# A written-out order of 2017 pieces laid anew, with another choice of engines

## The chip, the cores and the metric

One core of a Trainium2 chip. Times are device microseconds of one execution of the program on that core; lower is better. Five engines run side by side, each with its own list of instructions: TensorE (PE, matmuls, its weight loads shown as PEld), VectorE (DVE), ScalarE (ACT), GpSimd (POOL) and SyncE (SP), which here issues nearly all transfers.

## The reference

An attention over pooled keys and values feeds a layer that mixes tokens and channels. Eight batches, eight heads of 64, 576 tokens, float32:

```python
k_p = k.reshape(B, H, Sp, pool, D).mean(axis=3)      # pool = 8, Sp = 72
v_p = v.reshape(B, H, Sp, pool, D).mean(axis=3)
attn = softmax(scale * q @ k_p^T)
x = (attn @ v_p), heads side by side                 # 8 x 576 x 512
theta = x @ w_theta
zr, zi = x * cos(theta), x * sin(theta)
y = w_tok_r @ zr + w_tok_i @ zi                      # over the 576 tokens
u = x + y
out = u + maximum(u @ w_ch, 0)
```

(The softmax and the names are shortened; the weights come as 64-bit floats, which the kernel reads as pairs of 32-bit words.)

## The kernel before

The work of each batch is cut into streams, which are Python generators. One `next` of a stream records one piece: a transfer, a group of matmuls, or an elementwise step. A table, `SCHEDULE`, is a long list of words. Each word names a stream, with a letter behind it where the piece may run on more than one engine: v for VectorE, g for POOL, a for ScalarE. The loop at the end of the function takes the words one after the other and calls `next`. As every engine works through its list in the order in which pieces were recorded, the table sets the order on all engines and on SP's transfers, and the letter sets the engine. Nothing else decides it: the tiles' buffers are fixed by name, and waits follow from who wrote and who reads them.

The streams, with the batch as first number:
- `w`, `W`: the token weights, from 64-bit words to float pairs (`wsrc_a`, `wsrc_b`), then turned on TensorE into `WTh` and `WTl` (a value and its rounding error). `h` and `c` do the same for the angle weights `th`, `tl` and the channel weights `chh`, `chl`.
- `k`, `K`, `Q`, `v`, `V`: loads of keys, queries and values, pooling, and layout. SP issues 8 transfers for a later batch's `Q` piece, 2 for a `v` piece.
- `S`: scores of one token tile, maximum (L758), exponential (L779), sum, and the normalised weights `en`. From batch 2 on VectorE writes 32x32 transposed blocks into `G`.
- `E`: 16 transfers from `G` to `eraw` (L868) complete the transposition of a group of two or three token tiles; then a rounded copy `eh`, copies `er`, their errors, and the error of `eraw` in place (L889 on VectorE, L190 on POOL).
- `X`: the attention's product with the values, one channel block of 128 (`pv`, L916, four matmuls), and the copy that empties its PSUM bank into `xT` (L927 on VectorE, L925 on ScalarE). Most of these use one bank, so the next product waits for the copy.
- `T`: angles of one token tile (`pt`, L964), sine and cosine on ScalarE (L985, L993), and `z` (L1002, L1004).
- `Z`: `zh` and the rounding error `zl` of one channel block of `z` (L1036 on VectorE, L190 on POOL). `M`: the mix over tokens (`py`, L1056, 27 matmuls), the sum `xT` (L1066), and `uh`, `ul` (L1073 on VectorE, L190 on POOL).
- `F`: the product with the channel weights (`pf`, L1089, 12 matmuls), L1096, a transpose into `R` (L1109), and 4 transfers to the output.

Elementwise work on POOL goes through a helper (lines 190 and 194), which cuts a piece of 512 or more elements in two. Copies of every kind have the lines of another helper, 205 for ScalarE and 207 for VectorE and POOL. ScalarE holds one table of functions at a time, and the program puts an ACT_TABLE_LOAD wherever the next function is not in it: an exponential after a sine, or the other way round.

Of the kernel before, what the change touches and what calls it, by code (L numbers as in the profile page):

```python
# [35 lines left out]
w3.0 w0.1v X0.0.0v S0.2v w2.0 w1.1 w0.1 S0.4 S0.3v S0.2 X0.0.1 Q1.0 S0.2a Q1.1 X0.0.1v k1.1 h3v S0.2 w0.1 S0.4 h3
S0.3g h3 S0.3 X0.0.3 w2.1 k1.2 S0.3a w0.1v X0.0.3v w1.1 h3v S0.4 W0 X0.0.2 S0.2a h2v w2.0 S0.4g w1.1a w2.0a S0.3 h2
S0.3a X0.0.2v h1v S0.4g S0.4 S0.4a h3 h1 S0.4 Q1.0 w1.0g S0.4v w2.0a W0a K1.1g X0.2.3 h3v w1.1a h3 Q1.1 X0.2.3v
X0.2.1 W0 X0.2.1v T0.0a T0.0v Q1.1a T0.1a W0 w2.1 T0.0 v1.0 W0a w1.1 Q1.3 w2.1a T0.0 w2.0 X0.2.0 T0.1v w2.0 w2.1v
T0.0 X0.2.2 W0 T0.0 Q1.0a X0.2.0v w3.1 w1.1 w2.1 Q1.2 K1.2g T0.0 w1.1v W1 V1.0v T0.1 Q1.3 w2.1 T0.0a X0.2.2v T0.0  # L40
# [45 lines left out]
X4.0.1v S4.4 M3.0.1 X4.0.2 K6.0g Q5.1 X4.0.2v M3.0.0 Q5.1 X4.0.3 M3.0.1 M3.0.0 S4.4v X4.0.3v Z3.1v M3.0.1 K5a V5.2v
S4.4v M3.0.1 S4.4 X4.0.0 M3.1.0 M3.1.0 k6.1 M3.0.0v X4.0.0v S5.2 M3.0.1a M3.1.1 T4.0v M3.1.1 M3.1.1 T4.1a S5.2
Z3.3a S5.2 Z3.3v S5.2 M3.1.0 S5.2v S5.2v M3.1.1 T4.0v F2.2.1 Z3.2v S5.3 T4.1g M3.1.0 Z3.2g E4.2 K6.1g T4.0 M3.0.0v
T4.0 M3.0.1g M3.2.0 T4.0 S5.3 S5.3 E4.2a M3.2.0 M3.1.1g T4.0 M3.2.1 S5.2 M3.1.0g M3.2.1 M3.2.1 S5.3 S5.4 S5.3g T4.0
# [1156 lines left out]
```

## Time and profile before

| | before |
|---|---|
| median of 3 runs (584.72 to 588.34) | 585.06 us |
| profiled execution, its own time | 587.04 us |
| its span, first to last instruction | 585.3 us |
| busy: TensorE, VectorE, ScalarE, POOL | 558.0, 466.9, 322.5, 324.7 us |
| TensorE's mean granted clock | 0.994 |
| transfers | 57.84 MB, 99 GB/s |

A busy share tells how full an engine is, not what waits for what. For that the profile infers, for each instruction that began after idle time, who released it. TensorE's matmuls are pipelined: a matmul lasts longer than the distance to the next one, so times of work are read from runs of matmuls back to back. [...]

### The profile page before, as it was taken

To read this page: it belongs to the slowest core of one execution; us is meant where nothing else is said; L and a number is where in the kernel's file an instruction comes from. 1 tells how busy PE (TensorE), PEld (TensorE's weight loads), DVE (VectorE), ACT (ScalarE), POOL (GpSimd) and SP (SyncE) were. 2 spreads that over 40 slices of the span, in tenths; PEclk is the share of its full clock that TensorE was granted. 3 is DMA by queue.
4 is the path that set the end of the run, shared out by engine and by line. 5 is a ranking of instruction groups with operands and counts; after the bars stand their busy time and mean duration, and the time that the engine had idled before them with its cause. 6 is when DMAs were issued, how large, how long until landed. Compare 5 with 4: busy or idle time off the path is not lost.

```text
span 585.3 us, 11574 instructions
## 1 busy us (share of the span) xinstructions
PE 558.0 (95%) x4102; PEld 520.1 (89%) x4102; DVE 466.9 (80%) x931; ACT 322.5 (55%) x660; POOL 324.7 (55%) x476
## 2 busy tenths in 40 slices
PE   8899989998999988999999998999999999999997
PEld 7766989986899887899989897999899999999996
DVE  3989989898989888878887987888887987447345
ACT  3688958877952676536833562627633556425100
POOL 6435642455572586576746567276936785551250
PEclk9999989999999999999999998999999999999999
DMA  9966212367465667543365465316556151212115
GB/s 301 280 206 159 76 46 82 62 125 143 95 117 104 152 122 131 112 100 65 96 119 99 81 103 94 73 30 113 103 87 112 31 85 15 41 27 43 21 21 81
DMA packets 235385, 57.84 MB, mean 99 GB/s; under 512 B 223424, under 2 KB 223936, under 8 KB 235328
## 3 DMA queue, kind: packets, MB, share of 16 engines
q1 hardware_dynamic: 230464, 56.52, 46.8%
q10 hardware_dynamic: 4864, 0.59, 0.7%
q8 instruction: 32, 0.52, 0.4%
q14 instruction: 25, 0.20, 0.1%
HBM read 37.81 MB, written 9.44 MB: 81 GB/s over the span
## 4 chain that ended last, share of the span: by engine, by line
PE 45%; DVE 17%; SPq 11%; POOL 9%; ACT 8%; DMA 5%; issue 5%; DVEq 0%; POOLq 0%; ACTq 0%
PE py L1056 20%; SPq L868 8%; PE pt L964 8%; PE pf L1089 6%; PE pv L916 3%; SPq L601 3%; DMA vprst<-in_v_dram 2%; PE s L724 2%; DMA eraw<-G 1%; DMA qsst<-in_q_dram 1%; DVE qT L606 1%; POOL xl L190 1%; DVE xT L927 1%; DVE mx L758 1%; PE warm L308 1%
## 5 line engine op out<-in xcount | busy, mean ns | idle before, releaser
L1056 PE MATMUL py<-WTh,zh 128*128 128x288 f32 x576 | 83.3, 291 | 2.0 <-ACT zh L205 1.4
L1056 PE MATMUL py<-WTh,zl 128*128 128x288 f32 x576 | 81.8, 289 | 0.9 <-DVE xT L1066 0.5
L1056 PE MATMUL py<-WTl,zh 128*128 128x288 f32 x576 | 82.3, 287 | 0.0
L1056 PEld LDWEIGHTS py<-WTh,zh 128*128 128x128 f32 x576 | 75.5, 191 | 3.2 <-ACT zh L205 1.9
L1056 PEld LDWEIGHTS py<-WTh,zl 128*128 128x128 f32 x576 | 74.7, 189 | 1.9 <-POOL zl L190 0.8
L1056 PEld LDWEIGHTS py<-WTl,zh 128*128 128x128 f32 x576 | 75.1, 189 | 0.2
L190 POOL TENSOR_TENSOR zl<-z,zh 128x256 fp32r<-128x256 f32 (+2 forms) x57 | 44.5, 812 | 28.7 <-ACT zh L205 20.7
L970 ACT ACTIVATE g<-pt,c_magic 128x512 f32<-128x512 f32 x35 | 24.0, 685 | 64.8 <-PE pt L964 41.8
L190 POOL TENSOR_TENSOR ul<-xT,uh 128x288 fp32r<-128x288 f32 x37 | 32.2, 879 | 34.8 <-ACT uh L205 30.7
L1066 DVE TENSOR_TENSOR xT<-py,xT 128x288 f32<-128x288 f32 x64 | 28.5, 447 | 27.4 <-PE py L1056 27.2
L205 ACT CAST zh<-z 128x1152 fp32r<-128x1152 f32 (+1 forms) x29 | 30.8, 1075 | 28.6 <-PE py L1056 24.1
L1089 PE MATMUL pf<-uh,chh 128*128 128x288 f32 x256 | 43.6, 293 | 0.1
L190 POOL TENSOR_TENSOR en<-e_eps,ri 128x256 f32<-128x256 f32 (+3 forms) x62 | 31.5, 529 | 20.5 <-DVE ri L783 9.0
L1089 PE MATMUL pf<-ul,chh 128*128 128x288 f32 x256 | 42.1, 286 | 0.7 <-POOL ul L190 0.7
L724 PE MATMUL s<-kpT,qT 128*128 128x144 f32 x256 | 39.3, 295 | 3.2 <-DVE qT L207 1.5
L190 POOL TENSOR_TENSOR xl<-xT,xh 128x256 fp32r<-128x256 f32 x46 | 33.6, 751 | 15.5 <-ACT xh L205 10.7
L1089 PE MATMUL pf<-uh,chl 128*128 128x288 f32 x256 | 41.8, 286 | 0.0
L964 PE MATMUL pt<-th,xh 128*128 128x512 f32 x148 | 39.5, 389 | 2.2 <-DVE g L972 0.9
L724 PEld LDWEIGHTS s<-kpT,qT 128*128 128x128 f32 x256 | 34.8, 194 | 5.1 <-DVE qT L606 1.1
L964 PE MATMUL pt<-tl,xh 128*128 128x512 f32 x148 | 38.0, 379 | 0.0
L964 PE MATMUL pt<-th,xl 128*128 128x512 f32 x148 | 38.0, 379 | 0.0
L1089 PEld LDWEIGHTS pf<-uh,chh 128*128 128x128 f32 x256 | 36.1, 189 | 1.5 <-DVE xT L1096 0.5
(266 smaller groups left out, 1409.8 us busy)
## 6 DMA issues: line engine op xcount, KB each, us to landing
out_dram<-R SPq DMA_DIRECT2D x112, 72.0 KB, 2.2
kpst<-in_k_dram SPq DMA_DIRECT2D x15, 512.0 KB, 3.9
vpst<-in_v_dram SPq DMA_DIRECT2D x28, 256.0 KB, 3.7
qsst<-in_q_dram SPq DMA_DIRECT2D x96, 72.0 KB, 2.3
eraw<-G SPq DMA_DIRECT2D x96, 60.0 KB, 2.2
eraw<-G SPq DMA_DIRECT2D x96, 40.0 KB, 2.0
WTh_st<-in_moe_w_theta_dram SPq DMA_DIRECT2D x4, 512.0 KB, 8.3
wcraw<-in_moe_w_ch_dram SPq DMA_DIRECT2D x4, 512.0 KB, 3.3
```

Source lines behind the costliest of these rows:

```text
L190: nc.gpsimd.tensor_tensor(out[:, r], a[:, r], b[:, r], op)
L205: nc.scalar.copy(out, src)
L308: nc.tensor.matmul(p[:, 0:P], ident, ident, start=True, stop=True)
L601: nc.sync.dma_start(st[32 * i : 32 * i + 32, S * c : S * c + S].rearrange("p (x a) -> p x a", a=32), q[b, 4 * j + 2 * c + i // 2].rearrang ...
L724: nc.tensor.matmul(scs[c // 2][:n, 2 * SP * (c % 2) : 2 * SP * (c % 2 + 1)], qT[:, c, t0 : t0 + n], kpT[:, c, :], start=True, stop=True,)
L868: nc.sync.dma_start(blocks(Ex, jj, i), blocks(Gx, i, jj))
L916: nc.tensor.matmul(as_written(pv[:, :gn]) if pair else pv[:, :gn], l, by_turns(r) if pair else r, start=i == 0, stop=i == len(terms) - 1,)
L964: nc.tensor.matmul(as_written(pt), l[:, c, :], by_turns(r[:, c, :]), start=i == 0, stop=i == 11)
L970: nc.scalar.activation(halves(g), in_order(pt), AF.Identity, bias=c_magic)
L1056: nc.tensor.matmul(as_written(py[:, :n]), l[:, kk, :], by_turns(r[:, kk, t]), start=i == 0, stop=i == 3 * NK - 1,)
L1066: nc.vector.tensor_tensor(halves(u), in_order(py[:, :n]), halves(u), ALU.add)
L1089: nc.tensor.matmul(as_written(pv[:, :n]), l[:, kk, o], by_turns(uhl[r][:, kk, t]), start=i == 0, stop=i == 11,)
```

## The change

Only the table changes. The 2017 words are the same pieces; their order is another, and for 331 pieces the letter. The table is two lines shorter, so line numbers behind it are lower by 2 (L190 is L188 after). In counting the costs from which the new table was made, operations of VectorE and of POOL on SBUF were taken to exclude each other. The first line before and after:

```diff
-D k0.0 w0.0 K0.0 k0.1 K0.1 h0 w0.0 w0.0v w0.0g w0.0 K0.0a k0.2 K0.2 Q0.0 K0.2v h0 h0g K0.1v h0v h0 h1 w1.0 K0 K0a
...
+w0.0 w0.0 D k0.1 h0 k0.0 w0.0a k0.2 h0 w0.0v h0v K0.1 w0.0 K0.0 h0v h1 K0.0a K0.2 Q0.0 h2 K0.1a Q0.0 K0 Q0.1 w0.1 h0
...
```

Copies that empty the attention's banks (`X`) go from 57 on VectorE and 7 on ScalarE to 16 and 48. The `zl` pieces on POOL go from 57 to 77, on VectorE from 36 to 26. The error of `eraw` in 3 of the 12 `E` streams goes from POOL to VectorE.

POOL, at the end of the token weights. `wsrc_b` is the second float of a weight, `wcts` the channel weights' buffers, `wpow` a scratch buffer, `vpst` and `vp` values being pooled, and `Vl` their rounding error. Before:

```order
L190 TENSOR_TENSOR vpst1_1_860<-vpst1_1_860 128x256 x2
L190 TENSOR_TENSOR vpst1_1_860<-vpst1_1_860 128x2x128
L190 TENSOR_TENSOR vp1_688<-vpst1_1_860 128x128
L388 MEMSET wpow_115 128x512
L194 TENSOR_SCALAR wpow_115<-wcts0_898 128x256 x2
L190 TENSOR_TENSOR wsrc_b_155<-wsrc_b_155,wpow_115 128x288 x2
L190 TENSOR_TENSOR wcts0_898<-wcts0_898 128x256 x2
```

After:

```order
L188 TENSOR_TENSOR wsrc_b_120<-wsrc_b_120,wpow_115 128x288 x2
L386 MEMSET wpow_115 128x512
L188 TENSOR_TENSOR wsrc_b_120<-wsrc_b_120,eraw0_114 128x288 x2
L188 TENSOR_TENSOR wsrc_b_120<-wsrc_b_120,wpow_115 128x288 x2
L188 TENSOR_TENSOR Vl_916<-vp1_694,Vh_103 64x4x64 x2
L188 TENSOR_TENSOR wcts0_860<-wcts0_860 128x256 x2
L205 CAST chh_958<-wcts0_860 128x512
```

The two TENSOR_SCALAR ahead of the last `wsrc_b` have left POOL, the last three pieces of `wsrc_b` stand together, and a copy to `chh` has come in behind them.

POOL, the `E` stream of batch 5's second group (tokens from 256 on); `kprst` and `kpr` are keys of batch 6 being pooled, `vrx` and `Vr` the last value rows of batch 5. Before:

```order
L207 CAST eh5_256_4335<-eraw5_256_4334 128x1280
L190 TENSOR_TENSOR Vr5_4473<-vrx5_4327,mask_84 96x256 x2
L207 CAST er5_256_4336<-eraw5_256_4334 32x320 x4
L190 TENSOR_TENSOR kprst6_4382<-kprst6_4382 64x256
L190 TENSOR_TENSOR kprst6_4382<-kprst6_4382 64x128
L190 TENSOR_TENSOR kpr6_4513<-kprst6_4382 64x64
L190 TENSOR_TENSOR er5_256_4336<-eraw5_256_4334,er5_256_4336 32x320 x2
L190 TENSOR_TENSOR eraw5_256_4334<-eraw5_256_4334,eh5_256_4335 128x2x320 x2
```

After:

```order
L205 CAST eh5_256_4453<-eraw5_256_4452 128x1280
L188 TENSOR_TENSOR er5_256_4454<-eraw5_256_4452,er5_256_4454 32x320 x2
L188 TENSOR_TENSOR vrx5_4429<-vpr5_4031,vrh5_4430 32x64 x2
L188 TENSOR_TENSOR Vr5_4562<-vrx5_4429,mask_84 96x256 x2
L188 TENSOR_TENSOR eraw5_256_4452<-eraw5_256_4452,eh5_256_4453 128x2x320 x2
```

The four copies of `er` are on ScalarE now, the three sums of keys stand earlier, and two pieces of `vrx` have come in between.

SP, from the transfers of the `E` stream before that one (`eraw4`) to its own (`eraw5`). Before:

```order
L868 DMA eraw4_256_4051<-G_101 32x15x32 x16
L601 DMA qsst6_0_4224<-in_q_dram 32x18x32 x8
L1124 DMA out_0_dram<-R2_3_3780 32x18x32 x4
L515 DMA vpst6_0_4269<-in_v_dram 64x2x512 x2
L868 DMA eraw5_256_4334<-G_101 32x15x32 x16
```

After:

```order
L866 DMA eraw4_256_4057<-G_101 32x15x32 x16
L522 DMA kprst6_4177<-in_k_dram 64x512
L510 DMA kpst6_1_4256<-in_k_dram 128x2x512
L599 DMA qsst6_0_4356<-in_q_dram 32x18x32 x8
L1122 DMA out_0_dram<-R2_3_3876 32x18x32 x4
L1122 DMA out_0_dram<-R2_2_3837 32x18x32 x4
L513 DMA vpst6_0_4406<-in_v_dram 64x2x512 x2
L866 DMA eraw5_256_4452<-G_101 32x15x32 x16
```

Two loads of keys and four transfers to the output have come in between, 20 issues in place of 14.

ScalarE, the sine and cosine of batch 3's tile 1 (`g` the angle, `sn` the sine, `e_eps` the exponential of a softmax). Before:

```order
L970 ACTIVATE g3_1_3514<-pt3_1_3497,c_magic_88 128x512
L985 ACTIVATE sn3_1_3532<-g3_1_3514 128x512
L205 CAST uh2_3241<-xT2_2179 128x288
L988 ACTIVATE g3_1_3514<-g3_1_3514 128x512
L993 ACTIVATE g3_1_3514<-g3_1_3514,c_cos_92 128x512
```

After:

```order
L968 ACTIVATE g3_1_3502<-pt3_1_3473,c_magic_88 128x512
L983 ACTIVATE sn3_1_3541<-g3_1_3502 128x512
L986 ACTIVATE g3_1_3502<-g3_1_3502 128x512
L777 ACT_TABLE_LOAD
L777 ACTIVATE e_eps_99<-e_eps_99 128x8x72
L991 ACT_TABLE_LOAD
L991 ACTIVATE g3_1_3502<-g3_1_3502,c_cos_92 128x512
```

An exponential with its table has come between the two sines, and the sines' table is loaded again behind it. The same stands at tiles 0 and 1 of batch 4.

## Rows read from the trace of the kernel before

**Rows 1.** The page: the span, and busy time of each engine (us, share, instructions).

```profile
span 585.3 us, 11574 instructions
...
PE 558.0 (95%) x4102; PEld 520.1 (89%) x4102; DVE 466.9 (80%) x931; ACT 322.5 (55%) x660; POOL 324.7 (55%) x476
```

**Rows 2.** One stretch: its length, busy us of each engine, granted clock, DMA share.

```profile
15.00:240.00 225.00, 210.40 (x1497) 187.44 (x1498) 202.35 (x404) 163.39 (x411) 119.22 (x184) 0.99 0.57 126
```

**Rows 3.** Waits of TensorE, whole span: who for whom, total us, times, longest.

```profile
PE pv L916 <- DVE xT L927: 3.0, 3, 1.7
...
PE pv L916 <- POOL eraw L190: 2.1, 1, 2.1
...
PE wt L451 <- POOL wsrc_b L190: 1.4, 2, 0.9
```

**Rows 4.** Two stretches of 6 us, columns as in Rows 2.

```profile
76.00:82.00 6.00, 4.68 (x26) 4.22 (x26) 4.52 (x11) 3.17 (x9) 3.33 (x4) 0.72 0.27 90
356.00:362.00 6.00, 4.50 (x20) 4.06 (x21) 3.89 (x8) 1.34 (x4) 5.41 (x8) 0.72 0.32 49
```

**Rows 5.** Order of time, POOL from 72 to 78 us: start, us, engine, line, what.

```profile
72.75 0.53 POOL L388 MEMSET wpow<- 128x512 int32 x1 [1.24 <-DVE wpow L368]
...
73.36 2.16 POOL L194 TENSOR_SCALAR wpow<-wcts 128x256 f16<-128x256 f32 x2
...
75.61 2.31 POOL L190 TENSOR_TENSOR wsrc_b<-wsrc_b,wpow 128x288 fp32r<-128x288 f32 x2
```

**Rows 6.** Order of time, issues of the DMA queue, 316 to 345 us.

```profile
316.92 4.40 SPq L601 DMA_DIRECT2D qsst<-in_q_dram  x8
...
323.62 1.35 SPq L515 DMA_DIRECT2D vpst<-in_v_dram  x2
332.75 11.92 SPq L868 DMA_DIRECT2D eraw<-G  x16
```

**Rows 7.** Order of time, POOL, 346 to 358 us.

```profile
346.48 1.25 POOL L207 CAST eh<-eraw 128x1280 fp32r<-128x1280 f32 x1 [3.49 <-PE pf L1089]
...
348.82 1.92 POOL L207 CAST er<-eraw 32x320 fp32r<-32x320 f32 x4
350.81 1.25 POOL L190 TENSOR_TENSOR kprst<-kprst 64x256 f32<-64x256 f32 x2
...
354.40 3.04 POOL L190 TENSOR_TENSOR eraw<-eraw,eh 128x640 fp32r<-128x640 f32 x2
```

**Rows 8.** Order of time, TensorE, 226 to 229 us.

```profile
226.73 0.40 PE L916 MATMUL pv<-eh,Vh 128*128 128x320 f32 x1 [1.01 <-ACT eh L205]
...
228.26 0.40 PE L916 MATMUL pv<-eraw,Vh 128*128 128x320 f32 x1 [0.99 <-DVE eraw L889]
```

**Rows 9.** Chain that ended last: start, us, runs of matmuls back to back.

```profile
145.40 2.59 PE pt L964 x12
...
255.25 1.10 PE py L1056 x9
```

**Rows 10.** Groups: line, engine, what, count | busy us, mean ns | idle before.

```profile
L190 POOL TENSOR_TENSOR zl<-z,zh 128x256 fp32r<-128x256 f32 (+2 forms) x57 | 44.5, 812 | 28.7 <-ACT zh L205 20.7 <-DVE zh L207 5.4 <-PE py L1056 2.1
...
L1066 DVE TENSOR_TENSOR xT<-py,xT 128x288 f32<-128x288 f32 x64 | 28.5, 447 | 27.4 <-PE py L1056 27.2
...
L1036 DVE TENSOR_TENSOR zl<-z,zh 128x640 fp32r<-128x640 f32 (+1 forms) x36 | 26.1, 766 | 1.3 <-ACT zh L205 1.3
...
L927 DVE TENSOR_SCALAR xT<-pv 128x256 f32<-128x256 f32 (+1 forms) x57 | 25.3, 446 | 13.4 <-PE pv L916 12.7
L1109 DVE STREAM_TRANSPOSE R<-xT 128x288 f32<-128x288 f32 x56 | 24.9, 461 | 0.4
...
L985 ACT ACT_TABLE_LOAD x18 | 23.1, 1283 | 0.3
...
L1073 DVE TENSOR_TENSOR ul<-xT,uh 128x288 fp32r<-128x288 f32 x27 | 15.0, 566 | 0.1
...
L925 ACT ACTIVATE xT<-pv 128x320 f32<-128x320 f32 (+1 forms) x7 | 2.9, 420 | 6.6 <-PE pv L916 3.8 <-DVE mx L758 2.8
```

More of the change, by code (lines that the diff above doesn't have):

```diff
@@ L36 @@
[L36 to L40, printed above, removed]
@@ L86 @@
[L86 to L89, printed above, removed]
-E4.2a T4.0a E4.2v T4.0 S5.3g K6 M3.2.1 S5.4 T4.1 M3.2.0 E4.2g M3.1.1g M3.2.0 X4.2.0 S5.4 Q6.0 M3.3.0 X4.2.0v F2.3.1
@@ new lines @@
+X2.0.3 X2.0.3a S2.4 v3.1 K3a V3.2g M1.1.1 Z1.2g X2.0.0 Q3.1 X2.0.0a T2.0a T2.0v Z1.2v T2.1a M1.1.1 M1.1.1 S3.2 M1.1.1
+M1.0.1 T2.0 Z1.3a V3.1g E2.2 M1.1.1g S3.2 S3.2 k4.0 T2.1g M1.0.1v M1.2.0 T2.0 S3.2 M1.3.0 S3.2g T2.0 Z1.3v M1.3.0
+E2.2a S3.2v M1.0.0a M1.2.0 k4.2 S3.3 M1.2.0 S3.3 E2.2g M1.2.0 S3.3 E2.2g S3.2 M1.3.0 Q4.0 T2.0 M1.1.1g T2.1 M1.3.0
+F0.3.1 T2.0 F0.2.1 E2.2v S3.3 X2.2.0 T2.0a S3.3g S3.3v S3.4 T2.0 M1.2.1 S3.4 M1.0.0g M1.3.1 T2.0 X2.2.0a X2.2.2 S3.0
+S3.3 K4.2g M1.3.1 K4.0g X2.2.2v S3.4 S3.4 k4.1 T2.0 M1.2.0a M1.1.0g X2.2.3 T2.1 S3.4v T2.1 M1.3.1 S3.4g S3.4 X2.2.3a
@@ new lines @@
+T3.2 V4g T3.2 T3.2 Q5.1 F2.0.1 E4.0g E4.0g K5a T3.3 T3.3 F2.3.0 T3.3 v5.2 F2.1.0 S4.3g S4.3g T3.3 T3.3a F2.3.0 T3.3
+F2.2.1 F2.2.0 F2.1.1 T3.3 K5 F2.0.1 T3.3 V5.1g F2.1.1 F2.2.1 Z3.0a F2.2.0 E4.0g Z3.0g S4.3 S4.4 F2.3.1 M3.0.0 F2.2.1
+M3.0.0 S4.4 F2.3.1 F2.2.0 S4.4 X4.0.1 F2.0.1 Z3.1g M3.0.0 F2.3.0 F2.3.1 M3.0.1 Q5.1 k6.0 X4.0.1a K5a X4.0.2 X4.0.2v
+S5.2 S4.4g K6.0g S4.4g S4.4 M3.0.0 S5.2 M3.0.1 X4.0.3 X4.0.3a M3.0.1 M3.0.1 S5.2 Z3.1g X4.0.0 M3.1.0 M3.1.0 M3.1.1
+X4.0.0v M3.1.0 T4.0a T4.1v Z3.3v M3.1.1 M3.1.1 T4.1g T4.0g S5.3 V5.2g S5.2 Z3.2a S5.2g T4.0 E4.2 Z3.3v M3.1.0 S5.2g
@@ new lines @@
+Z3.2g M3.2.0 S5.3 M3.0.1v S5.3 S5.3 T4.0 T4.0 M3.2.0 S5.2 M3.2.0 E4.2v S5.3v E4.2a S5.4 M3.1.1 E4.2g S5.3g T4.1 M3.2.1
+E4.2v T4.0 k6.2 S5.4 X4.2.0 S5.0 T4.0 S5.3 M3.2.1 T4.0a X4.2.0v M3.1.0a X4.2.2 S5.4 M3.2.0 S5.4 X4.2.2v M3.2.1 S5.4v
+S5.4g M3.0.0a T4.0 S5.4 X4.2.3 S5.0 M3.3.0 k6.1 K6.1g M3.1.0v M3.0.1g X4.2.3a M3.2.1 X4.2.1 X4.2.1a M3.3.0 T4.2a
+M3.3.0 M3.2.1v X4.2.3a T4.3g T4.0 M3.0.0v T4.0 S5.0 M3.3.1 M3.3.0 M3.2.0a M3.3.1 T4.1 S5.0 T4.2g M3.2.1g M3.2.0v V5a
+T4.1 M3.3.0v S5.1 M3.1.1v M3.3.1 S5.0v M3.3.0v Q6.0 M3.3.1 S5.0v S5.1 F3.0.0 T4.1 F2.3.1 T4.1 S5.1 F2.2.1 K6.2g
@@ new lines @@
+M3.3.1a M3.1.1v v6.0 Q6.0 T4.1v T4.1 M3.3.1g F3.3.0 T4.1 V5g V5 F3.0.0 T4.3g T4.2 E5.2 T4.1 K6 T4.2 E5.2g F3.3.0 K6v
+F3.1.1 T4.2 T4.2 E5.2a T4.2 F3.0.1 F3.1.1 E5.2g F3.0.0 V5g F3.0.1 Q6.1 F3.0.1 S5.0 F3.0.1 F3.1.0 F3.1.0 F3.1.0 V5g
+F3.1.1 F3.1.1 T4.2a F3.3.1 T4.3 S5.1 T4.2 F3.3.1 T4.2 T4.2 F3.2.0 E5.2g F3.3.1 T4.3 Q6.1 F3.2.1 X5.2.2 T4.3 F3.2.0
+F3.3.0 F3.2.0 T4.3 K6 T4.3 F3.2.1 S5.1g T4.3a K6a F3.2.1 S5.1g S5.1 X5.2.2a X5.2.0 X5.2.1 X5.2.3 T4.3 X5.2.0a V6.0g
+T4.3 X5.2.1v X5.2.3a X5.2.3v T4.3 S6.0 T4.4a T4.4g Z4.0a Z4.0v S6.0 v6.1 T4.4 Z4.0v S6.0 E5.0 T4.4 M4.0.0 S6.0 Q7.0
@@ new lines @@
+k7.2 T5.0 M4.3.0 S6.3 S6.2v M4.3.1g T5.0v T5.1 M4.2.0 T5.0 T5.0 M4.3.0 T5.0 S6.3 T5.1 S6.3 M4.2.0 M4.2.1g S6.4 T5.1
+M4.3.1v M4.1.1v K7.1v M4.0.1v M4.2.0 T5.3a F4.1.1 M4.2.0 M4.2.0g T5.1 M4.2.0g T5.1 T5.1a T5.2 T5.1 V6g M4.0.0g F4.0.1
+T5.1 F4.1.1 K7 M4.3.0a T5.1 M4.3.0g V6 E6.0 v7.0 T5.2 Q7.0 T5.2 F4.0.1 T5.2 T5.3g T5.2 E6.0a F4.0.0 T5.2a F3.2.1 S6.2
+T5.2 T5.4g T5.2 S6.3 F4.0.0 T5.3 S6.3g E6.0a T5.2 E6.0g S6.3v F4.0.0 Q7.1 K7a F4.1.0 F4.3.1 F4.1.1 T5.3 T5.3 V6g
+F4.1.0 T5.3 T5.3 F4.0.1 V6g T5.3a F4.1.0 F4.3.1 F4.2.0 T5.3 K7.2g T5.3 T5.3 Z5.0a F4.2.1 F4.2.0 S6.3 F4.2.1 S6.4
@@ new lines @@
+F4.0.1 E6.0v S6.4 F4.3.0 K7 F4.3.0 F4.1.1 F4.2.1 F4.3.0 F4.2.0 Z5.0g K7a M5.0.0 M5.0.0 Z5.1g X6.0.2 S6.4 F4.3.1
+X6.0.2a M5.0.1 M5.0.1 S6.4v S6.4g M5.0.1 v7.2 S6.4 X6.0.1 Q7.1 Z5.1g M5.0.0 X6.0.1a X6.0.0 M5.0.1 S7.2 X6.0.0a M5.0.1g
+Z5.3g M5.0.0 X6.0.3 S7.2 X6.0.3a M5.1.0 F4.2.1 M5.1.1 S7.2 M5.1.1 Z5.3g T6.1g M5.1.0 S7.3 T6.0v S7.2 V7.0g V7.2g
+M5.0.1g S7.2v M5.1.0 M5.1.0 T6.0g M5.1.1 S7.2v M5.3.1 S7.3 E6.2 Z5.2a S7.3 S7.3 Z5.2g M5.3.1 E6.2a M5.1.0a M5.1.1
+F4.3.1 M5.3.1 T6.0 E6.2a M5.3.1 T6.1v S7.2 S7.3v M5.3.1v M5.3.0 S7.4 v7.1 S7.3g E6.2g M5.2.1 M5.2.1 M5.3.1v E6.2v
@@ new lines @@
+T6.1 T6.2 E7.2v S7.0g T6.2 F5.3.1 T6.2 F5.3.1 T6.2 T6.2a F5.3.0 F5.2.1 X7.2.3 F5.3.1 F5.3.0 T6.2 T6.3 X7.2.3v X7.2.1
+X7.2.1a T6.2 X7.2.2 F5.2.1 T6.2 T6.3 X7.2.0 X7.2.0a X7.2.2v T6.3 T6.3 X7.2.3v T6.3 T6.3a T6.4v T6.3 T6.4g S7.1 T6.3
+S7.0 T7.3a T6.3 Z6.0a Z6.0g T7.3g S7.1 T6.4 T6.4 T7.2a T6.4 T6.4 T6.4 T6.4v M6.0.0 T6.4 T6.4 Z6.0g S7.1 T7.2v T6.4
+M6.0.0 Z6.0g T7.3 Z6.1a M6.0.0 Z6.0v M6.0.1 M6.0.1 Z6.0g T7.3 S7.1 T7.3 T7.3 S7.1g T7.3 M6.0.1 S7.1g S7.1 M6.0.1
+M6.0.0 M6.0.0 T7.2 E7.0 M6.1.0 M6.0.1 Z6.1v M6.0.1g M6.1.0 Z6.3a M6.0.0v T7.3v M6.1.1 E7.0a M6.1.1 M6.1.0 Z6.3v M6.1.0
@@ L136 @@
+F7.3.1 F7.1.1 F7.1.1 F7.2.1 F7.1.1 F7.0.0 F7.2.1 F7.2.1 F7.2.0 F7.3.1 F7.3.0 F7.2.0 F7.2.0 F7.1.0 F7.2.1 F7.1.1 F7.2.0
+F7.3.0 F7.3.0 F7.1.0 F7.3.0 F7.1.0 F7.1.0
 """
```

159 lines of the change are left out of this document (65 added, 94 removed).

## The prediction

> **What bounds the kernel now.** Read the page's busy times first [rows 1]: TensorE is busy 558.0 of 585.3 us, so all that a new order can win is in the 27.3 us in which it stands, and in what the clock loses. No matmul is added or removed. VectorE comes next with 80%, ScalarE and POOL have 55% each. Then read where the idle time lies, in the stretches [rows 2]: from 15 to 240 us TensorE stands 14.6 us (225.00 less 210.40), and VectorE is busy 202.35 of 225.00, 90%, far above its mean. That part is held by both. Third, the waits of TensorE by releaser [rows 3]: none is over 3.0 us in total. They are many small late hand-overs: the attention's next product waits for the copy that empties its bank (VectorE, L927) and for the rounding error of the turned attention weights (`eraw`, by POOL here), and the turning of the token weights waits for POOL's `wsrc_b`. [...]
>
> What else the rows show: of two VectorE operations of one size, 128x288, the one with an input from PSUM takes 447 ns and the one with both inputs from SBUF 566 ns (L1066 and L1073) [rows 10]. [...]
>
> **The change part by part.** 2017 words stay 2017 words; what changes is their order and 331 letters. Counted in the built programs, VectorE's instructions go from 931 to 876, POOL's from 472 to 513, ScalarE's from 580 to 608, with ACT_TABLE_LOADs from 38 to 42.
>
> (a) The last token weights. Before, POOL clears a buffer (0.53 us) and makes two half tiles for the channel weights (2.16 us), and only then the last `wsrc_b` halves, 2.31 us [rows 5], for which TensorE waits 1.4 us [rows 3]; then comes the slow clock. After, the two half tiles go to ScalarE, and between the word for the last `wsrc_b` and the first word that turns it there are 18 warm-up matmuls, 16 of the previous turning and 8 transposes on TensorE, where before there were none. They are smaller than the 128x288 ones of 0.122 us [rows 9], so at most 42 × 0.122 = 5.1 us of cover, for a piece of 2.3. What is late next is the previous turning (W3): behind its last piece (`w3.1`) no matmul stands ahead of it. I take the whole of it: −1.4 −1.7 = **−3.1**; between −3.1 and nothing.
>
> (b) Turned attention weights of batch 3, second group (E3.2). TensorE waits 1.01 us for `eh` and 0.99 us for `eraw` [rows 8]. Between the last word of the softmax that feeds the turning and the first product, TensorE's own work was 48 `pf`, 24 `pt`, and 20 small ones; after, 96 `pf`, 24 `pt`, 18 `py` and 20 small ones. A matmul of 128x288 takes 1.10/9 = 0.122 us and one of `pt` 2.59/12 = 0.216 us [rows 9]. So 48 and 18 more are 66 × 0.122 = 8.1 us of cover more, against 2.0 of wait: **−2.0**; bounds −2.0 and nothing, if the DMA queue comes later by as much.
>
> (c) Batch 5, second group (E5.2). TensorE waits 2.1 us for POOL's `eraw` [rows 3] and loses 1.7 by the clock [rows 4]. The chain: 16 transfers issued in 11.92 us [rows 6], then POOL alone from 346.48 to 357.44 [rows 7]. On POOL the copies of `er` (1.92) go to ScalarE and the sums of `kprst` (1.25) go ahead of it; two small pieces come in, unpriced. On TensorE 27 `py` more stand in between, 27 × 0.122 = 3.3 us, and 12 small ones, at as much 1.4: 4.7 us more cover. On the DMA queue, 20 issues stand between this stream's transfers and those of the E stream before it, where 14 stood: 6 more, at 4.40/8 = 0.55 us each 3.3 us [rows 6]. Before, the queue stood idle 7.8 us (from 323.62 + 1.35 to 332.75) until the softmax was done, so they fit in, if the keys' load at their head finds its buffer free early. Then nothing of the wait is left (2.1 − 4.7 − 1.9 − 1.2 < 0). If it does not, all 20 issues, 11.0 us, fall behind the softmax, and the wait grows to 2.1 + 11.0 − 4.7 − 1.9 − 1.2 = 5.3 us. Bounds: −3.8 and +3.2. The idle 7.8 us make the first the nearer one; I take half of its gain: **−1.9**.
>
> (d) Emptying the attention's banks. 41 of VectorE's 57 copies go to ScalarE: 41 × 0.446 = 18.3 us off the fuller engine, 41 × 0.420 = 17.2 us on one that is busy 55% [rows 1, 10]. TensorE waits 3.0 us for them [rows 3]. On ScalarE they stand behind casts and table loads as well, so I take half: **−1.5**, from −3.0 to nothing.
>
> (e) Four more table loads. Each is 1.283 us [rows 10]. Three come because an exponential is put between the two sines of one tile (T3.1, T4.0, T4.1). Cover: ScalarE is idle 45% of the time, and these tiles' `z` is wanted later. All on the path would be 5.1 us, none 0; I take half of one load, **+0.7**.
>
> (f) More rounding errors on POOL. `zl` pieces on POOL go from 57 to 77, on VectorE from 36 to 26: five more channel blocks. One takes POOL 4 × 0.812 = 3.2 us, VectorE 2 × 0.766 = 1.5 us [rows 10]. The product first does 18 matmuls without `zl`, 18 × 0.122 = 2.2 us of cover, so 1.0 us can show in each: up to 5.2, down to 0. No wait on `zl` is among the larger ones of before although 57 pieces were there, so I take a quarter: **+1.3**.
>
> (g) Late places of its own. [...] Another order will have some too that I can't name; I charge half of one: **+1.9**, from 0 to two of them, 6.9.
>
> Sum: −3.1 −2.0 −1.9 −1.5 +0.7 +1.3 +1.9 = −4.6 us. The profiled execution's span is 585.3 us and its own time 587.04, 1.7 us around the span; that gives 580.7 and 582.4. The median of the runs shown is 585.06, 2.0 below the profiled one; with the same −4.6 it becomes **580.4 us**.
>
> **The rivals.**
> VectorE's relief comes through. Weighted with the durations of before, VectorE's list sums to some 20 us less, 18 of them in (d), and the fuller part of the kernel is 15 to 240 us. If VectorE is what TensorE waits for there, two thirds of the 14.6 us of idle time go, 9.7, with the clock's 1.7 and (c)'s 1.9; less 2.0 for (e) and (f): −11.3, 573.8 us. For it: 90% busy. Against it: the rows of waits name POOL and ScalarE too, and POOL is handed 41 instructions.
>
> The waits only change places. TensorE's waits are spread over many releasers, and a new order draws all of them anew; an order that also keeps apart operations that the rows show not to disturb each other (transposes) gives away freedom for nothing. Then the change does not do what it says, and the time is 585 us, give or take 2.
>
> POOL becomes the late engine: slower. It gets 20 `zl`, 12 `vpst` and 3 `ul` pieces more, each about twice as long as on VectorE. [...] The trace agrees, 3.2 us against 1.5 for a block. The place is the product of the channel blocks: all five of (f) show, 5.2 us, and two of them are long enough to take the clock down, 2 × 1.7; (b), (c) and (d) are lost since their chains run through POOL, (a) stays, (e) adds 0.7: 5.2 + 3.4 + 0.7 − 3.1 = +6.2, 591.3 us. It decides once POOL starts a `zl` more than the 2.2 us of cover less its own 3.2 allow, that is at once in these blocks. Against it: POOL's share rises only from 55% to about 60%.
>
> **How the numbers follow.** Forecast (−8 to −2) 0.45; VectorE's relief 0.20; waits change places 0.22; POOL late 0.13. About 1% of this kernel, 5.9 us, is what a measurement can tell from no change: faster means under 579.2, slower over 590.9. Faster: all of the relief, and 0.20 of the forecast's 0.45, since 580.4 lies close to the line: 0.40. Slower: 0.12 of POOL's 0.13. Same: 0.48. The range, from the relief's 573.8 to just under POOL's 591.3, is 573.5 to 590.0, with 2 in 10 left out, more of it above. The forecast's own range is 577 to 583.
>
> **What would show it.** After: TensorE idle near 23 us instead of 27.3. (a) no wait for `wsrc_b` of over 0.5 and a clock of 1.00 around the last turning. (b) no wait for `eraw` before the product of batch 3's second group. (c) no wait of over 1 us at batch 5's, the clock not down, and its transfers issued as soon as the softmax is done. (d) waits for L927's copy under 1.5, none as long for ScalarE's L923. (e) `g` of T3.1 to T4.1 late, TensorE not. (f) waits for `zl` under 1.5 in sum. The prediction is wrong if VectorE's busy time does not fall, if a gap of 2 us opens at E5.2 behind the DMA queue, or if more than two falls of the clock are seen between 15 and 560 us.

## The result, and the profile after

| | before | after |
|---|---|---|
| median, 13 executions each | 585.87 us | 578.60 us |
| ratio, 95% interval | | 0.9873, 0.985 to 0.9896 |
| again, later (21 and 9 executions) | 584.54 us | 579.94 us; 0.9915, 0.9885 to 0.9945 |
| profiled execution, its own time | 587.04 us | 575.52 us |
| its span | 585.3 us | 573.7 us |
| busy: TensorE, VectorE, ScalarE, POOL | 558.0, 466.9, 322.5, 324.7 us | 550.3, 467.5, 328.6, 357.2 us |
| TensorE's mean granted clock | 0.994 | 0.998 |

The change makes the kernel 4.6 to 7.3 us faster, about 1%. (Ratios leave disturbed executions out, so they can differ a little from those of the medians.) The profiled execution is the fastest of its 13, and in it the clock did not fall before the last matmul (1.00 in every stretch up to 567.0 us, 0.84 behind it); over 22 executions the mean granted clock is 0.992, over 50 of the kernel before 0.9935. So the clock, which gives 3.4 us between the two profiles, gives nothing between the medians.

The page after, beside [rows 1]:

```profile
span 573.7 us, 11562 instructions
...
PE 550.3 (96%) x4102; PEld 516.0 (90%) x4102; DVE 467.5 (81%) x876; ACT 328.6 (57%) x688; POOL 357.2 (62%) x517
```

TensorE stands 23.5 us in place of 27.2 (unrounded; the page's rounded figures give 23.4 and 27.3). VectorE has 55 instructions fewer and is busy as long as before; that is explained below. The stretches of [rows 2] and of the first row of [rows 4], in the same columns:

```profile
15.00:240.00 225.00, 216.11 (x1580) 195.18 (x1580) 204.56 (x391) 173.48 (x435) 148.61 (x214) 1.00 0.62 129
76.00:82.00 6.00, 4.55 (x39) 4.17 (x38) 5.80 (x14) 4.81 (x8) 2.29 (x4) 1.00 0.08 29
```

From 15 to 240 us TensorE stands 8.9 us in place of 14.6. From 76 to 82 us the clock stays up, but TensorE still stands 1.45 us. The waits of TensorE, in the columns of [rows 3], say for what:

```profile
PE py L1054 <- ACT zh L203: 2.5, 3, 1.5
PE pv L914 <- ACT xT L923: 2.2, 5, 0.7
PE pt L962 <- ACT xh L203: 1.7, 2, 1.2
...
PE s L722 <- DVE qT L604: 1.3, 1, 1.3
PE pq L627 <- DMA early<-in_q_dram: 1.3, 1, 1.3
PE pv L914 <- DVE eraw L887: 1.1, 1, 1.1
PE kpp L566 <- DMA kpst<-in_k_dram: 0.8, 1, 0.8
PE wt L446 <- DVE WTl L457: 0.7, 1, 0.7
...
PE py L1054 <- POOL zl L188: 0.2, 1, 0.2
```

The three releasers of [rows 3] are gone: no `wsrc_b`, no `eraw` by POOL, no bank copy of VectorE. New places of 1 to 1.5 us stand in the list instead: the cast `zh` at 77 us, `xh` at 131, `qT` at 417, `eraw` by VectorE at 439, a first load of queries at 19.

The account of the 11.5 us (unrounded) between the two spans, the time behind the last matmul (the tail) apart:

| | before | after | |
|---|---|---|---|
| waits that steps (a) to (d) name (1.4, 2.0, 2.1, 3.0) | 8.5 | 2.2 | −6.3 |
| all other idle time of TensorE | 14.4 | 14.5 | +0.1 |
| lost to a low clock before the last matmul | 3.4 | 0 | −3.4 |
| tail | 4.3 | 6.8 | +2.5 |
| TensorE's busy time without the clock (558.0 − 3.4; 550.3) | 554.6 | 550.3 | −4.3 |

The last line is short stalls which the profile shows as busy, since no matmul was added or removed: matmuls overlap in it (in the kernel before one of `py` lasts 287 to 291 ns in the mean, and back to back they come 0.122 us apart). They aren't in the waits, but the trace has them by tile: counted without the clock, the attention's product `pv` makes 1.8 us of them, 1.6 in the first matmul of a product, the one that needs an emptied bank; `pe` makes 0.9, `s` and `pf` 0.7 each. The idle time falls in the same place. The two groups of `pv` that wait, before and then after, in the columns of [rows 10]:

```profile
L916 PE MATMUL pv<-eh,Vh 128*128 128x256 f32 (+1 forms) x56 | 18.1, 324 | 4.8 <-DVE xT L927 3.0 <-ACT eh L205 1.0 <-DVE er L836 0.7
L916 PE MATMUL pv<-eraw,Vh 128*128 128x256 f32 (+1 forms) x56 | 16.5, 295 | 4.3 <-DVE eraw L889 2.2 <-POOL eraw L190 2.1
```

```profile
L914 PE MATMUL pv<-eh,Vh 128*128 128x256 f32 (+1 forms) x56 | 17.6, 315 | 2.3 <-ACT xT L923 2.2
L914 PE MATMUL pv<-eraw,Vh 128*128 128x256 f32 (+1 forms) x56 | 16.2, 289 | 1.1 <-DVE eraw L887 1.1
```

In front of these two the idle time falls from 9.1 to 3.4 us. That is 5.7 of the 6.2 us by which TensorE's idle time before its last matmul falls (22.9 to 16.7).

### The profile page after: what moved, and what is told of

The parts are those of the page before. It is cut to its first block, busy times and chain, and to the rows that moved or that the text cites. A ratio compares the mean times of both kernels' runs of the same rounds, so it can differ in the third digit from the quotient of the medians.

```text
span 573.7 us, 11562 instructions
## 1 busy us (share of the span) xinstructions
PE 550.3 (96%) x4102; PEld 516.0 (90%) x4102; DVE 467.5 (81%) x876; ACT 328.6 (57%) x688; POOL 357.2 (62%) x517
## 4 chain that ended last, share of the span: by engine, by line
PE 56%; DVE 18%; DMA 7%; SPq 6%; ACT 5%; POOL 4%; issue 3%; DVEq 0%; ACTq 0%; POOLq 0%
PE py L1054 22%; PE pf L1087 11%; PE pt L962 10%; SPq L866 5%; PE pv L914 4%; PE s L722 3%; DMA kpst<-in_k_dram 2%; DVE en L784 2%; PE px L976 2%; ACT e_eps L765 1%; DMA eraw<-G 1%; DMA early<-in_q_dram 1%; DVE mx L756 1%; DVE R L1107 1%; DVE z L1002 1%
## 5 line engine op out<-in xcount | busy, mean ns | idle before, releaser
L1054 PE MATMUL py<-WTh,zh 128*128 128x288 f32 x576 | 82.0, 288 | 3.0 <-ACT zh L203 2.5
L188 POOL TENSOR_TENSOR zl<-z,zh 128x256 fp32r<-128x256 f32 (+2 forms) x77 | 62.1, 835 | 23.3 <-DVE zh L205 15.0
L1064 DVE TENSOR_TENSOR xT<-py,xT 128x288 f32<-128x288 f32 x64 | 28.1, 446 | 31.9 <-PE py L1054 31.6
L188 POOL TENSOR_TENSOR en<-e_eps,ri 128x256 f32<-128x256 f32 (+3 forms) x68 | 36.8, 560 | 26.0 <-DVE ri L781 20.7
L188 POOL TENSOR_TENSOR ul<-xT,uh 128x288 fp32r<-128x288 f32 x40 | 33.3, 841 | 25.6 <-DVE uh L205 18.8
L923 ACT ACTIVATE xT<-pv 128x256 f32<-128x256 f32 (+1 forms) x48 | 19.4, 409 | 47.0 <-PE pv L914 40.6
L722 PE MATMUL s<-kpT,qT 128*128 128x144 f32 x256 | 37.6, 289 | 1.6 <-DVE qT L604 1.3
L1094 DVE SCALAR_TENSOR_TENSOR xT<-pf,xT 128x288 f32<-128x288 f32 x64 | 28.2, 444 | 9.7 <-PE pf L1087 8.8
```

The lines of the kernel that those rows point to most:

```text
L188: nc.gpsimd.tensor_tensor(out[:, r], a[:, r], b[:, r], op)
L722: nc.tensor.matmul(scs[c // 2][:n, 2 * SP * (c % 2) : 2 * SP * (c % 2 + 1)], qT[:, c, t0 : t0 + n], kpT[:, c, :], start=True, stop=True,)
L923: nc.scalar.activation(x, pv, AF.Copy, scale=1.0 / POOL)
L1054: nc.tensor.matmul(as_written(py[:, :n]), l[:, kk, :], by_turns(r[:, kk, t]), start=i == 0, stop=i == 3 * NK - 1,)
L1064: nc.vector.tensor_tensor(halves(u), in_order(py[:, :n]), halves(u), ALU.add)
L1094: nc.vector.scalar_tensor_tensor(halves(oT), in_order(pv[:, :n]), 0.0, halves(oT), ALU.max, ALU.add)
```

## Experiments

Ratios are to the kernel before, on the same chip.

### Nothing changed

> The kernel before, unchanged, as a measure of what the comparison can tell and to see the granted clock of several of its executions. Every theory expects a ratio of 1.000, at most 0.3% off. The times of the changed kernel ran from 575.5 to 581.2 us with mean clocks from 0.998 to 0.990, so its spread looks like the clock's falls (each 3.41 us at half clock, 1.7 us lost). If that is the cause of the spread here too, time less the loss, (1 - clock) x span, is the same in all executions within 1 us, near 583.6 us.

585.56 us, 0.9974 (0.9946 to 1.0002). The clocks of its 12 executions ran from 0.987 to 0.997, the times from 583.1 to 589.2. So 0.3% is what a comparison can be off. The spread goes with the clock in part only: time less the clock's loss was expected within 1 us, near 583.6, and runs from 579.7 to 584.3.

> The changed kernel, unchanged, on the chip of the next two kernels. Its median was 578.6 us with a mean clock from 0.999 to 0.985. In the two kernels made from it, TensorE waited 1.7 to 2.1 us for transfers of keys and queries before 24 us, and the clock fell there for 6.83 us once or twice (3.4 us lost each). If these waits vary from execution to execution and make the spread, the unchanged kernel shows such falls before 60 us in its profile or clocks of 0.985 to 0.99 in its runs, with a median of 578 to 581 us.

579.94 us. The profiled execution waits longer for the first loads. TensorE's waits:

```profile
PE kpp L566 <- DMA kpst<-in_k_dram: 1.9, 1, 1.9
PE pq L627 <- DMA early<-in_q_dram: 1.8, 1, 1.8
```

The stretch in which its clock falls, (1 − 0.69) × 11 = 3.4 us:

```profile
45.00:56.00 11.00, 10.70 (x36) 7.17 (x36) 9.47 (x17) 7.34 (x16) 3.95 (x5) 0.69 0.59 149
```

The new order waits on transfers at its start, and how long differs between executions (0.8 and 1.3 us in the first profile). That fits the spread; that these waits bring each fall isn't shown.

The profiles of before_again and after_again, from two chips, repeat the account with the clock the other way. The spans are 583.0 and 578.1 us; idle time before the last matmul gives −3.8, the clock +1.7, the tail +2.4 and the short stalls −5.1.

### Order and engines apart

The table has two parts, the order of the words and their letters. Each was taken alone. A word keeps its place and takes the letter of the other table, for all 331:

```diff
-c0a ... W4v ... X7.0.1a
+c0g ... W4a ... X7.0.1v
```

> The new order of the pieces, but each piece on the engine that it had before. Theory 1 (the gain is late hand-overs that the new order removes, and the clock falls behind them): most of the 7.3 us stays, 579 to 582 us; the copies of the attention's banks that are VectorE's again cost 0 to 3 us. Theory 2 (VectorE's relief, by the letters): the gain is gone, 585 us or more, because VectorE has its 41 copies back. Theory 3 (order and engines only work together, as the pieces were laid with the durations of the new engines): new waits of 1 to 2 us at several places, 584 to 590 us.

643.44 us, 1.0973 (1.093 to 1.1016).

> The old order of the pieces, each piece on its new engine. Theory 1 (order): 583 to 587 us, with the waits for the turned attention weights of batch 3 and of batch 5 still there. Only the wait for wsrc_b (1.4 us) goes, since that piece is freed by a letter. Theory 2 (VectorE's relief by the letters): most of the gain comes, 577 to 580 us. Theory 3 (they only work together): slower than both, 588 us or more.

647.96 us, 1.0996 (1.0945 to 1.1047). Neither half holds any of the gain; each costs 57 to 61 us. The longest waits of TensorE, of the new order with old engines first, then of the old order with new ones:

```profile
PE pv L914 <- DVE xT L925: 12.0, 11, 2.8
PE pf L1087 <- POOL ul L188: 7.7, 3, 3.2
```

```profile
PE pv L916 <- POOL eraw L190: 4.7, 2, 4.4
PE py L1056 <- DVE xT L1066: 4.6, 4, 2.8
```

All engines take part. This is theory 3 of the expectations: an order fits the engines for which it was laid. Its size was missed by far, as it expected 584 to 590 us for the first of the two. Theories 1 (order) and 2 (letters) both fall here.

### The bank copies alone, both ways

Of the `X` pieces only the copies (second word) change engine, 44 one way and 3 the other.

```diff
-X0.0.0a  (after)
+X0.0.0v
-X0.0.0v  (before)
+X0.0.0a
```

> The changed kernel, only the copies that empty the attention's banks back on the engines of before (41 net from ScalarE to VectorE). Theory 1: they matter only where TensorE waits for them; VectorE's copy is 0.446 us and ScalarE's 0.409, so each costs about the same, and the time is 578 to 581 us (0 to +3 by waits behind VectorE's longer list). Theory 2 (VectorE's relief): 18 us more on VectorE, 583 to 586 us, and VectorE's busy time near 486 us.

598.44 us, 1.0144 (1.008 to 1.0208). Against 0.9915 and 0.9873 that is 13 to 16 us slower than the changed kernel. Both theories missed it: the time is 12 us above the higher of them, and VectorE's busy time 8 us below what the second expected. The page, and then TensorE's longest wait:

```profile
PE 556.9 (94%) x4102; PEld 518.9 (87%) x4102; DVE 477.9 (80%) x917; ACT 314.2 (53%) x647; POOL 357.2 (60%) x517
```

```profile
PE pv L914 <- DVE xT L925: 14.0, 12, 2.6
```

> The kernel before, its order untouched, only the copies that empty the attention's banks on the engines that the change gives them (41 net from VectorE to ScalarE). Theory 2 (VectorE's relief: 41 x 0.446 = 18 us off the fuller engine): most of the change's gain, 575 to 581 us. Theory 3 (an order only fits the engines for which it was laid: in ScalarE's list the copies stand behind casts, activations and table loads that the old order put there): TensorE waits for L925's copies by 10 us or more, 592 to 600 us. Taking them back in the new order cost 12 to 20 us; theory 2 says that the same step gains here, theory 3 that it costs here too.

593.16 us, 1.0138 (1.0113 to 1.0164). The same two views:

```profile
PE 561.5 (95%) x4102; PEld 524.6 (89%) x4102; DVE 450.8 (76%) x890; ACT 335.8 (57%) x701; POOL 323.8 (55%) x476
```

```profile
PE pv L916 <- ACT xT L925: 5.0, 4, 1.9
```

This is the clean test of VectorE's relief in the old order. Its busy time, 466.9 and 468.9 us in two profiles of the kernel before, falls to 450.8, near the 41 × 0.446 = 18.3 us of the copies, and the kernel is 8 us slower: in ScalarE's list the copies stand where the old order put them, behind other work. (Some 3 of the 8 us are clock, 0.988 in the mean against 0.993.) A fuller engine was made emptier, and it bought nothing. after_x_back shows the other side: TensorE waits 14.0 us for copies that stand in VectorE's list at the places laid for ScalarE's. The waits that theory 3 expected for before_x_moved (10 us or more) were too many, its time right.

### Two letters of the change in the old kernel

```diff
-T0.4 T0.3 c0g T0.4 T0.3
+T0.4 T0.3 c0a T0.4 T0.3
-F3.0.0 S5.1 E5.2g T4.2
+F3.0.0 S5.1 E5.2a T4.2
```

> The kernel before with two letters of the change alone: the two half tiles for the channel weights that stand ahead of the last wsrc_b go from POOL to ScalarE, and the four copies of er of batch 5's second group go from POOL to ScalarE. By steps (a) and (c) of the prediction: the wait for wsrc_b (1.4 us) is gone, and the wait for eraw at 355 us (2.1) shrinks by up to 1.9, each with its fall of the clock (1.7): 579 to 583 us in all. Theory 3: ScalarE is at its sines and table loads at 345 to 351 us, so the copies of er come no earlier there and the second wait stays at 1.5 to 2.5 us; 583 to 586 us.

583.71 us, 0.9978 (0.9957 to 0.9999), against 0.9974 for no change: nothing that can be told apart, and less than the 2 to 6 us of steps (a) and (c). But the places answer. TensorE's wait at the first:

```profile
PE wt L451 <- POOL wsrc_b L190: 0.8, 1, 0.8
```

ScalarE at the second, in order of time:

```profile
342.70 1.90 ACT L205 CAST er<-eraw 32x320 fp32r<-32x320 f32 x4 [2.72 <-DMA eraw<-G]
```

The stretches of both places, with the clock behind the busy times:

```profile
76.00:82.00 6.00, 5.05 (x39) 4.26 (x38) 4.85 (x11) 4.24 (x10) 2.96 (x4) 1.00 0.26 90
350.00:360.00 10.00, 9.49 (x61) 8.28 (x59) 9.43 (x19) 3.88 (x7) 7.72 (x10) 1.00 0.55 85
```

The wait for `wsrc_b` falls from 1.4 to 0.8 us, POOL's `eraw` (2.1, and 1.7 in before_again) is no longer among the waits, and both clocks are 1.00. In before_again the clock fell at 79 us (0.99 from 15 to 240 us), not at 356 (1.00 from 240 to 555), so only the first says something, and here it fell at 136 us instead (0.996 over the span). ScalarE was free at 342.70, before its sines, so theory 3 was wrong about this place, though its time (583 to 586 us) was right: here one letter did its work in the old order, and 2.7 us less of two waits bought at most 2.5 us of time.

### Places of the changed kernel

(e), the three exponentials between two sines, here for one of them:

```diff
-S4.3 S4.4 M2.2.1v M2.2.0g M2.2.0g T3.1 T3.1 V5.0g
+T3.1 S4.3 S4.4 M2.2.1v M2.2.0g M2.2.0g T3.1 V5.0g
```

> The changed kernel with the three exponentials that stand between the two sines of T3.1, T4.0 and T4.1 moved behind the second sine, so that fewer ACT_TABLE_LOADs of 1.28 us are needed. If table loads lie beside other work (ScalarE is busy 57%): 578 to 579 us, no change. If they are on the path, as step (e) half assumed: 0.7 to 3 us less. If the exponentials are wanted sooner than the cosines (theory 3, the order is tight there): 1 to 3 us more.

581.65 us, 0.9936 (0.9908 to 0.9964). Only two table loads went (688 instructions on ScalarE became 686), and the kernel isn't faster: no sign that table loads, 1.28 us each, are on the path. The third view (1 to 3 us more) fits the time as well, and 0.3% can't tell it from no change.

The `qT` transpose and the last transfers:

```diff
-M5.0.1 S6.4v S6.4g M5.0.1 v7.2 S6.4 X6.0.1 Q7.1
+M5.0.1 Q7.1 S6.4v S6.4g M5.0.1 v7.2 S6.4 X6.0.1
-M7.1.0v M7.3.1 ... M7.1.1v F6.2.0 M7.3.1g ... F6.2.1
+M7.1.0v F6.2.0 F6.2.1 M7.3.1 ... M7.1.1v M7.3.1g ...
```

> The changed kernel with two places moved in its order. First, the last transpose of batch 6's output and the 4 transfers behind it go ahead of the last sums, so that these transfers are not issued within 2 us of the first transfers of batch 7. Second, the transpose into qT of batch 7's second half goes ahead of the 64x512 product (L784) that stands 3.77 us on VectorE while POOL works off four zl halves back to back (3.10 us). If the tail of 6.8 us after the last matmul (4.3 before) comes from these late transfers, it becomes 4.3 to 5 us. If the wait of 1.35 us for qT comes from the stretched L784, it goes, and L784 ends no later. Both: 574 to 576.5 us. If neither: 578.5 us.

579.87 us, 0.9899 (0.9857 to 0.994): no change that can be told, in an execution whose clock was low at the start (0.86 from 15 to 65 us). The first place, VectorE and POOL in order of time (start, us), changed kernel and then this one:

```profile
412.63 3.77 DVE L784 TENSOR_TENSOR en<-e_eps,ri 64x512 f32<-64x512 f32 x1
417.19 1.33 DVE L604 STREAM_TRANSPOSE qT<-qsst 128x1152 f32<-128x1152 f32 x1
...
412.76 3.10 POOL L188 TENSOR_TENSOR zl<-z,zh 128x384 fp32r<-128x384 f32 x4
```

```profile
420.44 1.33 DVE L604 STREAM_TRANSPOSE qT<-qsst 128x1152 f32<-128x1152 f32 x1
421.69 2.50 DVE L784 TENSOR_TENSOR en<-e_eps,ri 64x512 f32<-64x512 f32 x1
...
420.56 3.09 POOL L188 TENSOR_TENSOR zl<-z,zh 128x384 fp32r<-128x384 f32 x4
```

L784 ends 0.5 us behind POOL's last `zl` in both (416.40 and 415.86; 424.19 and 423.65), so it takes 3.77 or 2.50 us as it starts earlier or later. The transpose takes 1.33 us beside POOL as without it, and TensorE's wait for `qT` is gone. The second place did not answer: the tail stays at 6.7 us, so the nearness of these transfers to the last ones is not its reason.

> The changed kernel with the qT transpose ahead of L784 (as before) and the last transposes and transfers of batch 6's block 2 some 25 pieces earlier. Built this way, the completion counters of the last 32 transfers alternate: SP's transfers use four of the eight, ScalarE's queue the other four, as in the kernel before. In the changed kernel they mix, and SP's first transfer of batch 7 shares its counter with the second one of ScalarE's queue; SP stands 2.2 us until that has landed (559.30 to 561.49 us). If the mixing of counters makes the longer tail, it falls from 6.7 to 4.3 us and the time by 2.4 us. If the tail comes from the number of transfers near the end, it stays at 6.7.

579.50 us, 0.9913 (0.9878 to 0.9948). The diff is as above, with the three `F6.2` pieces behind `Z7.3v`. The last transfers of the changed kernel, of after_two_moves, and of this one, by queue:

```profile
559.27 9.71 ACTq L1112 DMA_DIRECT2D out_dram<-rz  x16
561.87 9.78 SPq L1112 DMA_DIRECT2D out_dram<-rz  x16
```

```profile
565.70 9.71 ACTq L1112 DMA_DIRECT2D out_dram<-rz  x16
568.23 9.81 SPq L1112 DMA_DIRECT2D out_dram<-rz  x16
```

```profile
564.65 9.57 SPq L1112 DMA_DIRECT2D out_dram<-rz  x16
564.66 9.77 ACTq L1112 DMA_DIRECT2D out_dram<-rz  x16
```

Both queues issue 16 transfers in 9.6 to 9.8 us. In the first two SP begins 2.5 to 2.6 us late, and in the built program SP's first transfer waits on the completion counter that the second transfer of ScalarE's queue has (2.2 us, SP's longest wait for a transfer there in the changed kernel); here both begin together, and the tail falls to 5.0 us (4.3 was expected). But TensorE gets a new wait; VectorE and TensorE in order of time:

```profile
551.38 0.84 DVE L1107 STREAM_TRANSPOSE R<-xT 128x288 f32<-128x288 f32 x2 [3.30 <-DMA out_dram<-R]
...
552.62 1.37 PE L1054 MATMUL py<-WTh,zl 128*128 128x288 f32 x9 [1.95 <-DVE xT L1064]
```

The transposes, moved ahead of the last sums, stand 3.30 us for the buffer `R` that earlier transfers still read, and with them VectorE's next sum, for which TensorE waits 1.95 us. The tail's 1.7 us have changed places.

> As after_tail, and at the start the first load of token weights goes behind the first keys, and the second one behind the queries' third tile, as TensorE waits there for keys and queries (0.8 to 2.0 and 1.3 to 2.1 us). If these waits bring the clock falls before 60 us, they shrink to under 1 us each and the runs' clocks rise to 0.993 or more: 572 to 576 us. If ScalarE and VectorE then wait for the token weights instead, the same time is lost a little later: same as after_tail, or 1 to 3 us more.

578.06 us, 0.99 (0.9869 to 0.9932). The wait for the queries is gone, `kpst` is still waited for by 1.4 us and ScalarE's copy of `kp` newly by 1.7. The clocks rose in part, as the first view has it: 9 of 12 executions at 0.993 or more, 3 of 7 in after_tail. But the profile's clock still falls at 15 and 80 us (0.96 from 15 to 60 us, 0.99 from 60 to 240), and the time is no clear gain on after_tail. None of these versions beats the changed kernel by more than a measurement can tell.

Last, POOL's pieces whole:

```diff
-            if n < 512:
+            if n < 1 << 20:
```

> The changed kernel, but POOL's helper no longer cuts a piece in two, so that one instruction of POOL does what two did (zl of a block in two instead of four). In the changed kernel three VectorE operations (xl 128x512 at 431.1 us, en 64x512 at 412.6, uh 128x288 at 300.9) took 3.77, 3.77 and 2.45 us and ended just behind four zl halves that POOL did back to back, though POOL began a new instruction three times in between. [...] If VectorE could get in between two instructions of POOL, whole pieces make VectorE wait longer: more operations of VectorE stretched by over 0.5 us (18 now), and 582 us or more.

579.88 us in 4 executions, 0.9865 (0.9802 to 0.9929): no change in time that can be told. POOL's busy time falls from 357.2 to 335.2 us. The three VectorE operations took 2.96, 3.51 and 1.86 us and ended 0.2 to 0.6 us behind the last `zl`, as in the changed kernel, though two of them are 0.6 and 0.8 us shorter than there. But 29 VectorE operations instead of 18 are stretched by over 0.5 us, as expected if VectorE gets in between two instructions of POOL; the 582 us or more that went with it did not come. So between two instructions of POOL VectorE gets in at times, not always. The changed kernel's own trace agrees: of 50 VectorE operations stretched by over 0.2 us, 42 ended behind the first POOL instruction that ended during them, 8 behind a later one.

## Why the prediction was right, and where its steps were not

The forecast was −4.6 us and its own range 577 to 583; the medians say −7.3 and −4.6. By steps:

(a) Half. The 1.7 us for the clock, here and in (c), is (1 − 0.72) × 6 [rows 4]: in the kernel before the granted clock was 0.50 from 78 to 81 us and from 358 to 361. The wait for `wsrc_b` is gone. The step asked what would be late next and named the previous turning; that is late by 0.7 us (`WTl` at 75 us), but TensorE also waits 1.5 us for `zh`, the cast of `z`, in the same 76 to 82 us. In three other profiles of the new order (after_tail, after_tail_head, after_whole) the clock still falls at 80 us (0.99 from 60 to 240 us in the first two, 0.987 over the span in the third), so the 1.7 us are kept only in some executions.

(b) Right: at this product (215.57 us) no wait for `eh` or `eraw`, only 0.7 us for a bank copy within it. The 2.0 us are one execution's: in before_again the same two waits were 1.3.

(c) Right in mechanism, half in size. Taken at half of 3.8, it came whole (in before_again the wait was 1.7 us, with no fall of the clock). The softmax's last write to `G`, the transfers, ScalarE's copies and POOL's error, as in [rows 6] and [rows 7]:

```profile
316.29 0.19 DVE L803 STREAM_TRANSPOSE G<-en 64x64 f32<-64x64 f32 x1
...
316.77 1.30 SPq L513 DMA_DIRECT2D vpst<-in_v_dram  x2
318.23 10.71 SPq L866 DMA_DIRECT2D eraw<-G  x16
329.04 5.66 SPq L599 DMA_DIRECT2D qsst<-in_q_dram  x8
...
332.75 1.88 ACT L203 CAST er<-eraw 32x320 fp32r<-32x320 f32 x4
...
337.78 3.06 POOL L188 TENSOR_TENSOR eraw<-eraw,eh 128x640 fp32r<-128x640 f32 x2
```

The product began at 342.57 us, 1.7 after the error was done. The feared gap behind the queue came small: the 20 issues ahead of the stream's own end at 318.07, 1.6 us after the softmax, and the cover held.

(d) Waits of 3.0 us became 2.2: −0.8 for −1.5. With the short stalls of a product's first matmul, which the step did not count, it is −2.4. The reason behind it (VectorE relieved) was not right: the copies are worth nothing without the order that goes with them.

(e) and (f) cost nothing: no `g` among the waits, 0.2 us for `zl`. The 2.0 us charged for both were too much; the cover held.

(g) was the weakest step. Its 1.9 us are half of 3.8, a wait of 2.1 [rows 3] and the 1.7 of the clock. No run shows how long a wait has to be for such a fall: 1.4 and 2.1 us came with one in the kernel before, 1.7 us in before_again and the 1.45 us from 76 to 82 in the changed kernel with none. It charged new places and nothing for old ones that vanish. Both happened: idle time that no step names is 14.4 us before and 14.5 after. And the two clock falls of before, 3.4 us, of which the sum took 2.5, come back elsewhere: the mean clock hardly differs, and six of the seven profiles that keep the new letters and nearly all of the new order have falls of their own, in the first 55 us or at 80 us (mean clocks 0.985 to 0.993 in these six). What stands against these, −4.3 us of short stalls and +2.5 of tail, no step had.

So the place was right, the attention's product, and the letters and order that free it; that the sum came so near is in part luck. It has 2.5 us of clock that the medians don't show and 2.0 us of costs in (e) and (f) that did not come, charges 1.9 in (g) without the old places that go, and lacks the short stalls and the tail.

The sentence that the prediction is wrong if VectorE's busy time does not fall came true: 466.9 and 467.5 us. The time fell all the same, so that sentence was wrong. Busy time counts the time for which an operation is held beside POOL (L784 3.77 us, undisturbed 0.68). Taking for each form the time over its lower quartile, where that is more than 0.06 us, 48 operations were stretched by 16.3 us in sum before, 67 by 33.1 after. All of the 67 ran beside POOL for over 30% of their time, and 45 of the 48. Without the stretching VectorE's busy time falls by 16.2 us, from 450.6 to 434.4: the relief came, and the stretching took it back. (The 119 ns between the prediction's 566 and 447 ns, L1073 and L1066, are such stretching too: in the kernel before either takes 0.45 us while POOL is idle, and L1073 takes 0.71 on average when POOL works beside it for over half of its time.) The new order doesn't keep two-input operations of the two engines apart; it was laid with their stretching in the count. That this is why its hand-overs come on time is argued, not shown: no run had an order laid without it.

Of the rivals, VectorE's relief as a cause by itself is refuted by before_x_moved, and 573.8 us was not reached; in the new order the same copies are worth 13 to 16 us. That the waits only change places holds for the idle time that no step names and for the small repairs tried, not for the attention's product. POOL as the late engine did not come: 62% busy, 0.2 us of waits beside the 1.4 at the start that both kernels have. That two waits for `zl` would take the clock down, 2 × 1.7, was the author's estimate.

## What to carry to other kernels

In a written-out order the place and the engine of a piece are one decision: moving 41 copies off the fuller engine cost 8 us in the old order and was worth 13 to 16 in the new one. Count a gain by the waits that end at named places, and for the rest assume that as many new ones open; a repair of one place has to show what its engine and its buffer wait for next. Don't count on a clock fall that one execution shows.
